# Decay of q moved to the eviction of x^T, weight conversion split over two engines, weight loads paced, second halves of w1 and w2 converted beside the FFN, a group's conversions moved behind the next scores

## The chip, the cores and the metric

One core of a Trainium2 chip. The metric is the device time of one execution in microseconds (us). "Span" is an execution seen by the profiler, 1.6 to 2.2 us shorter than its time (3.5 once).

The engines: TensorE (PE in the profile, PEld its weight loads), VectorE (DVE), ScalarE (ACT), GpSimd (POOL), and SyncE (SP), which here only issues DMAs. "SPq" is SyncE's own instruction queue.

## The reference, cut to what matters

```python
# q, k, v: (8, 8, 576, 64) fp32.   w1, w2: (512, 1024), w3: (1024, 1024), w_out: (1024, 512), all fp64
gamma = 1.0 - 2.0 ** (-5.0 - np.arange(H))
Dmat  = np.where(rel >= 0, gamma[:, None, None] ** rel, 0.0)       # rel = query position - key position
attn  = np.matmul(scale * np.matmul(q, k^T) * Dmat, v)             # linear attention with decay
x     = attn.transpose(0, 2, 1, 3).reshape(4608, 512)
a, b  = x @ w1, x @ w2
out   = ((a * b) @ w3) @ w_out
```

The weights come as fp64 and the kernel computes in fp32, so it rebuilds fp32 numbers from the two 32-bit words of each fp64 value. w3 and w_out have nothing between them, so the kernel multiplies them once: w3o = w3 @ w_out.

## The kernel before

Two stages. In the first, 20 groups (four pairs of batch entries, five chunks of up to 128 positions each) go through attention, and beside it 40 blocks of 128 x 512 weights are loaded as raw fp64 (0.52 MB each), converted, and w3 @ w_out is formed. In the second, the FFN runs over 12 tiles of 384 rows.

The decay is split: k's side multiplies v, q's side multiplies q, both on GpSimd, before TensorE transposes q and k.

```python
def load(g, names):                    # k, q, v of a chunk; pieces of 256 bytes
    ...
        t = ld.tile([P, 2 * H, D], F32, tag="ld_" + nm, bufs={"k": 2, "q": 1, "v": 3}[nm])
        nc.sync.dma_start(t[:sz], src[nm][...])

def front(g):
    for t, gam in ((qn, gq), (vn, gk)):
        nc.gpsimd.tensor_tensor(out=t[:sz], in0=t[:sz], in1=gam[...].to_broadcast([sz, 2 * H, D]), op=ALU.mult)
    # transposes of k and q on TensorE, evicted by ScalarE
    ...
def load_block():                      # a raw fp64 block; three buffers
    t = raw.tile([P, CV, 2], I32, tag="raw", bufs=3)
    nc.sync.dma_start(t, w[...])       # the same SyncE queue as k, q, v
    ...
def convert_block():                   # seven VectorE operations
    ...
    converted[0] += 1
    load_block()                       # refills the buffer that was just freed

for g in range(G):                     # G = 20
    load(g + 2, "kv")
    front(g + 1)
    load(g + 2, "q")
    w3_work(...)                       # transposes and products of w3 that are ready
    convert_up_to(pace[g])             # 2 or 3 blocks a group
    pv(g)                              # attention product, evicted to x^T by ScalarE
    state(g + 1)
    score(g + 1)                       # scores; VectorE multiplies them with the causal mask
```

In the timelines of this case VectorE's operations, and the loads in SyncE's queue, start in the order of the program (those of the changed kernel at 36 to 51 us are shown below).

## Time and profile before

| | |
|---|---|
| time, median (range) | 1050.91 us (1049.49 to 1051.23) |
| first stage / FFN | 303.6 / 746.4 us |
| TensorE busy, first stage | 234.8 us, mean granted clock 0.88 |
| VectorE busy, first stage | 236.5 us |
| share of the 16 DMA engines, first stage | 0.76, at 164 GB/s |

To read it: no engine is full over the first stage as a whole, so the stage is made of stretches with different bounds. The lines are in the prediction below (there and later, a row of 40 digits is the span in 40 equal slices, and a digit the busy share in tenths; PEclk is the granted clock in tenths of full speed; a DMA share can pass 1, as it adds up the times of packets; a line of waits ends with total us, times, and the longest wait).

### The profile page before, as it was taken

The numbers are of one execution on the slowest core, as the hardware profiler recorded it, in microseconds if no ns is written. First come the engines' busy times: TensorE is split into PE (matmuls) and PEld (weight loads), VectorE is DVE, ScalarE is ACT, GpSimd is POOL, SyncE is SP. The second block draws the span as 40 slices with busy tenths as digits, with TensorE's granted clock in tenths as the row PEclk, the third lists the DMA queues.
The fourth block names the chain that finished last, engine by engine and source line by source line (L and its number), as shares of the span: only waits on it lengthen the run. The fifth ranks groups of instructions, "written<-read, shape, count | busy, mean of one in ns | idle before, by whom it ended". The sixth has DMA issues, their size and how long they took to land.

```text
span 1050.1 us, 11351 instructions
## 1 busy us (share of the span) xinstructions
PE 977.6 (93%) x4933; PEld 582.6 (55%) x4933; DVE 290.0 (28%) x475; ACT 146.7 (14%) x285; POOL 82.7 (8%) x47
## 2 busy tenths in 40 slices
PE   3974999886799999999999999999999999999998
PEld 3853655575675455554555555455554545555453
DVE  4898679599821000010100001010010101001010
ACT  2322121232220000000000010000101000000010
POOL 3333121223310000000000000000000000000000
PEclk8887999987899999999999999999999999999999
DMA  9976576699900000000000000000000000000000
GB/s 191 241 164 153 129 160 149 133 213 185 174 4 1 21 10 1 30 1 31 0 13 17 1 30 1 31 0 11 20 1 31 0 21 10 11 20 1 31 0 30
DMA packets 124002, 59.51 MB, mean 57 GB/s; under 512 B 114216, under 2 KB 114216, under 8 KB 123952
## 3 DMA queue, kind: packets, MB, share of 16 engines
q1 hardware_dynamic: 122624, 58.73, 24.0%
q8 instruction: 38, 0.62, 0.3%
q10 hardware_dynamic: 1328, 0.06, 0.1%
q14 instruction: 12, 0.10, 0.0%
HBM read 49.34 MB, written 9.44 MB: 56 GB/s over the span
## 4 chain that ended last, share of the span: by engine, by line
PE 78%; DVE 18%; issue 2%; DMA 1%; SPq 1%; ACTq 0%; ACT 0%; POOL 0%; POOLq 0%; DVEq 0%
PE up L352 47%; PE po L363 24%; PE ps L298 3%; DVE e L267 3%; DVE pm L152 3%; DVE m L272 3%; DVE e L262 2%; DVE e L264 2%; DVE e L265 2%; DVE m L270 2%; DVE w L274 1%; PE xps L197 1%; DVE w_sb L274 1%; PE tp L134 1%; PE tp L290 1%
## 5 line engine op out<-in xcount | busy, mean ns | idle before, releaser
L352 PE MATMUL up<-xT,w_sb 128*128 128x384 f32 x1536 | 497.4, 486 | 0.0
L352 PEld LDWEIGHTS up<-xT,w_sb 128*128 128x128 f32 x1536 | 291.8, 190 | 205.8 <-issue 5.4
L363 PE MATMUL po<-w3o,ab 128*128 128x512 f32 x576 | 249.2, 592 | 0.0
L357 DVE TENSOR_TENSOR ab<-up,a 128x384 f32<-128x384 f32 x96 | 53.5, 558 | 670.6 <-PE up L352 670.6
L363 PEld LDWEIGHTS po<-w3o,ab 128*128 128x128 f32 x576 | 109.4, 190 | 135.2 <-issue 132.0
L356 ACT COPY a<-up 128x384 f32<-128x384 f32 x96 | 46.0, 479 | 416.6 <-PE up L352 416.6
L134 PE MATMUL tp<-ident,ld_q 128*128 128x128 f32 (+1 forms) x160 | 26.7, 311 | 55.6 <-POOL ld_q L123 35.1
L298 PE MATMUL ps<-wo,w3T 128*128 128x512 f32 x128 | 59.6, 622 | 0.0
L366 ACT COPY ot<-po 128x512 f32<-128x512 f32 x36 | 21.1, 586 | 258.9 <-PE po L363 258.9
L123 POOL TENSOR_TENSOR ld_q<-ld_q,gq 128x1024 f32<-128x1024 f32 (+1 forms) x20 | 40.5, 2025 | 207.6 <-DMA ld_q<-in_q_dram 195.6
L152 DVE TENSOR_TENSOR pm<-sc,mask 128x512 f32<-128x512 f32 (+1 forms) x80 | 45.3, 626 | 36.2 <-PE sc L149 36.2
L134 PEld LDWEIGHTS tp<-ident,ld_q 128*128 128x128 f32 (+1 forms) x160 | 20.0, 166 | 60.6 <-POOL ld_q L123 37.9
L197 PE MATMUL xps<-pm,ld_v 128*64 128x128 f32 (+1 forms) x640 | 42.8, 296 | 0.0
L123 POOL TENSOR_TENSOR ld_v<-ld_v,gk 128x1024 f32<-128x1024 f32 (+1 forms) x20 | 42.0, 2101 | 2.9 <-DMA ld_v<-in_v_dram 2.9
L298 PEld LDWEIGHTS ps<-wo,w3T 128*128 128x128 f32 x128 | 25.2, 202 | 29.5 <-issue 29.2
L197 PEld LDWEIGHTS xps<-pm,ld_v 128*64 128x64 f32 (+1 forms) x640 | 38.2, 160 | 5.3 <-issue 5.3
L149 PE MATMUL sc<-qT,kT 64*128 64x128 f32 (+1 forms) x640 | 40.3, 278 | 0.0
L149 PEld LDWEIGHTS sc<-qT,kT 64*128 64x128 f32 (+1 forms) x640 | 36.6, 188 | 1.6 <-issue 0.5
L267 DVE SCALAR_TENSOR_TENSOR e<-raw,e 128x512 int32<-128x512 int32 x40 | 32.4, 811 | 1.4
L272 DVE SCALAR_TENSOR_TENSOR m<-raw,m 128x512 f32<-128x512 uint32 x40 | 29.3, 732 | 1.4
L262 DVE TENSOR_SCALAR e<-raw 128x512 int32<-128x512 int32 x40 | 29.2, 729 | 0.8
L137 ACT COPY qT<-tp 128x512 f32<-128x512 f32 (+1 forms) x40 | 21.3, 550 | 56.7 <-PE tp L134 56.7
(32 smaller groups left out, 307.1 us busy)
## 6 DMA issues: line engine op xcount, KB each, us to landing
raw<-in_moe_w_dram SPq DMA_DIRECT2D x24, 512.0 KB, 4.3
out_dram<-ot SPq DMA_DIRECT2D x36, 256.0 KB, 2.0
ld_k<-in_k_dram SPq DMA_DIRECT2D x16, 512.0 KB, 6.0
ld_v<-in_v_dram SPq DMA_DIRECT2D x16, 512.0 KB, 8.4
ld_q<-in_q_dram SPq DMA_DIRECT2D x16, 512.0 KB, 7.1
raw<-in_moe_w_out_dram SPq DMA_DIRECT2D x8, 512.0 KB, 4.9
raw<-in_moe_w_dram SPq DMA_DIRECT2D x16, 256.0 KB, 5.4
ld_k<-in_k_dram SPq DMA_DIRECT2D x4, 256.0 KB, 4.8
```

Of the source, the lines that this page charges most:

```text
L123: nc.gpsimd.tensor_tensor(out=t[:sz], in0=t[:sz], in1=gam[:sz, c].rearrange("p b h -> p (b h)").unsqueeze(2).to_broadcast([sz, 2 * H, D]), ...
L134: nc.tensor.transpose(tp[:, p, :sz], src[:sz, h:h + 2, :].rearrange("p a d -> p (a d)"), ident[:sz, :sz])
L149: nc.tensor.matmul(sc[j][:sz, p, :sz], kT[hs, b, p, :sz], qT[hs, b, p, :sz], start=True, stop=True)
L152: nc.vector.tensor_mul(pm[:sz, b, j, :, :sz], sc[j][:sz, :, :sz], mask[:sz, :sz].unsqueeze(1).to_broadcast([sz, NP, sz]))
L197: nc.tensor.matmul(banks[r][heads[half], b, n, :sz], vs[:sz, b * H + 2 * p + j, :], pm[:sz, b, j, p, :sz], start=(c == 0 and m == 0), stop ...
L262: vec.tensor_scalar(out=e, in0=hi, scalar1=1, scalar2=21, op0=ALU.logical_shift_left, op1=ALU.logical_shift_right)
L267: vec.scalar_tensor_tensor(e, in0=hi, scalar=-(1 << 31), in1=e, op0=ALU.bitwise_and, op1=ALU.bitwise_or)
L272: vec.scalar_tensor_tensor(m.bitcast(F32), in0=lo.bitcast(U32), scalar=2.0 ** -32, in1=m, op0=ALU.mult, op1=ALU.add)
L298: nc.tensor.matmul(ps, live["w3T", ft][:, g, :], wo[:, g, :], start=(g == 0), stop=(g == KF - 1))
L352: nc.tensor.matmul(t, w[:, c, f * P:(f + 1) * P], xT[:, c, n * TB:(n + 1) * TB], start=(c == 0), stop=(c == KD - 1))
L357: nc.vector.tensor_mul(live["ab", i, n][:, f, :], ps[1], a)
L363: nc.tensor.matmul(po, ab[:, f, t * P:(t + 1) * P], w3o[:, f, :], start=(f == 0), stop=(f == KF - 1))
```

## The change

Its intent: take the multiplication of q off GpSimd (and off the way to TensorE), make VectorE's conversion cheaper, and move part of it out of the first stage.

- GpSimd no longer multiplies q. The decay of q, spread over partitions by eight small TensorE products, is applied when x^T is evicted from PSUM (the memory that TensorE writes its products to), which VectorE now does instead of ScalarE.
- Two of the seven conversion operations become two relus on ScalarE. To let them overlap, a block is begun one ahead of the one being finished.
- The pacing puts 8 blocks into the first 11 groups and 24 into the last 9. The last 8 of the 40 (second halves of w1 and w2) are converted beside the first FFN products.
- The w3 product is cut in two parts around the attention product, and a group's conversions move behind the next group's scores.

```diff
 def front(g):
-    for t, gam in ((qn, gq), (vn, gk)):
-        nc.gpsimd.tensor_tensor(out=t[:sz], in0=t[:sz], in1=gam[...], op=ALU.mult)
+    nc.gpsimd.tensor_tensor(out=vn[:sz]..., in0=vn[:sz]..., in1=gk[...], op=ALU.mult)
 ...
 def pv(g):
-        nc.scalar.copy(live["xT", i][...], banks[r][:, :, :, :sz])
+        nc.vector.tensor_tensor(out=live["xT", i][...], in0=banks[r][:, :, :, :sz], in1=gT[...], op=ALU.mult)
 ...
-    vec.tensor_scalar(out=e, in0=e, scalar1=-896.0, scalar2=0.0, op0=ALU.add, op1=ALU.max)
-    vec.tensor_scalar(out=e, in0=e, scalar1=255.0, scalar2=2.0 ** 23, op0=ALU.min, op1=ALU.mult)
+    nc.scalar.activation(e, e, relu, bias=lim[:, 0:1], scale=-1.0)
+    nc.scalar.activation(e, e, relu, bias=lim[:, 1:2], scale=-2.0 ** 23)
 ...
+    slow, few = G // 2 + 1, KF
+    first = len(blocks) - 2 * KD
+    pace = [few * (g + 1) // slow for g in range(slow)]
+    pace += [few + -(-(first - few) * (g + 1) // (G - slow)) for g in range(G - slow)]
 ...
+    load(0, "kqv")          # now ahead of everything else
 ...
     score(0)
+    decays()                # eight products that spread the decay of q
     for g in range(G):
         load(g + 2, "kv")
         front(g + 1)
         load(g + 2, "q")
-        w3_work((converted[0] - KF) // 2)
-        convert_up_to(pace[g])
+        w3_mm(done, 0)
         pv(g)
+        w3_mm(done, 1)
         state(g + 1)
         score(g + 1)
+        w3_tr(turned[0])
+        convert_up_to(pace[g])
 ...
+    for half in range(2):
+        for n in range(2):
+            for f in range(half * NP, half * NP + NP):
+                up(0, n, f)
+                convert_up_to(converted[0] + 1)
```

More of the change, by code (lines that the diff above doesn't have):

```diff
@@ L73 @@
     w3_part, first_part = ExitStack(), ExitStack()
-    wst = w3_part.enter_context(tc.tile_pool(name="wst", bufs=2))
-    raw, ld, fr = (first_part.enter_context(tc.tile_pool(name=nm, bufs=2, side="right"))
-                   for nm in ("raw", "ld", "fr"))
+    raw = ctx.enter_context(tc.tile_pool(name="raw", bufs=2, side="right"))
+    wst = w3_part.enter_context(tc.tile_pool(name="wst", bufs=1))
+    ld, fr = (first_part.enter_context(tc.tile_pool(name=nm, bufs=2, side="right")) for nm in ("ld", "fr"))
     ctx.enter_context(tc.manual_schedule())
-    ident = const.tile([P, P], F32, tag="ident", name="ident")
-    make_identity(nc, ident)
-    mask = const.tile([P, P], F32, tag="mask", name="mask")
-    nc.vector.memset(mask, 1.0)
-    nc.gpsimd.affine_select(out=mask, in_=mask, compare_op=ALU.is_ge, fill=0.0,
-                            base=0, pattern=[[1, P]], channel_multiplier=-1)
-    gk = const.tile([P, NC, 2, H], F32, tag="gk", name="gk")
-    gq = const.tile([P, NC, 2, H], F32, tag="gq", name="gq")
-    dq = const.tile([H, S], F32, tag="dq", name="dq")
-    nc.scalar.dma_start(dq, decay_q)
-    for c in range(NC):
-        for b in range(2):
-            nc.scalar.dma_start(gk[:sizes[c], c, b, :], decay_k[starts[c]:starts[c] + sizes[c], :])
-    gps = acc.tile([P, NC, H], F32, tag="acc", name="gps")
-    for c in range(NC):
-        nc.tensor.transpose(gps[:sizes[c], c, :], dq[:, starts[c]:starts[c] + sizes[c]], ident[:H, :H])
-    for c in range(NC):
-        for b in range(2):
-            nc.vector.tensor_copy(gq[:sizes[c], c, b, :], gps[:sizes[c], c, :])
-    w1_sb = const.tile([P, KD, DF], F32, tag="w1", name="w1_sb")
-    w3o = const.tile([P, KF, DM], F32, tag="w3o", name="w3o")
-    wo = wst.tile([P, KF, DM], F32, tag="wo", name="wo", bufs=1)
     live = {}
@@ L116, in load, with decays @@
             live[nm, g] = t
+    load(0, "kqv")
+    ident = const.tile([P, P], F32, tag="ident", name="ident")
+    make_identity(nc, ident)
+    mask = const.tile([P, P], F32, tag="mask", name="mask")
+    nc.vector.memset(mask, 1.0)
+    nc.gpsimd.affine_select(out=mask, in_=mask, compare_op=ALU.is_ge, fill=0.0,
+                            base=0, pattern=[[1, P]], channel_multiplier=-1)
+    gk = const.tile([P, NC, H], F32, tag="gk", name="gk")
+    dq = wst.tile([P, DF], F32, tag="w3", name="dq")[:H, :S]
+    nc.scalar.dma_start(gk[:short, 0, :], decay_k[:short, :])
+    nc.scalar.dma_start(gk[:, 1:, :], decay_k[short:, :].rearrange("(c p) h -> p c h", p=P))
+    nc.scalar.dma_start(dq, decay_q)
+    gT = const.tile([P, NP, S], F32, tag="gT", name="gT")
+    lim = const.tile([P, 2], F32, tag="lim", name="lim")
+    nc.vector.memset(lim[:, 0:1], 1151.0)
+    nc.vector.memset(lim[:, 1:2], 255.0 * 2.0 ** 23)
+    def decays():
+        sel = wst.tile([P, KF, P], F32, tag="w3T", name="sel")
+        for p in range(NP):
+            for half in range(2):
+                h = 2 * p + (half ^ (p // 2))
+                nc.vector.tensor_copy(sel[:H, p, heads[half]], ident[:H, h:h + 1].to_broadcast([H, D]))
+        for s0 in range(0, S, S // 2):
+            for p in range(NP):
+                gps = acc.tile([P, S // 2], F32, tag="acc", name="gps")
+                nc.tensor.matmul(gps, sel[:H, p, :], dq[:, s0:s0 + S // 2],
+                                 start=True, stop=True)
+                nc.scalar.copy(gT[:, p, s0:s0 + S // 2], gps)
+    w12h = {nm: [const.tile([P, KD, CV], F32, tag=nm + "a", name=nm + "_sb")] for nm in ("w1", "w2")}
+    w3o = const.tile([P, KF, DM], F32, tag="w3o", name="w3o")
+    wo = wst.tile([P, KF, DM], F32, tag="wo", name="wo")
     def front(g):
@@ L121, in front @@
         kn, qn, vn = live["k", g], live["q", g], live["v", g]
-        for t, gam in ((qn, gq), (vn, gk)):
-            nc.gpsimd.tensor_tensor(
-                out=t[:sz], in0=t[:sz],
-                in1=gam[:sz, c].rearrange("p b h -> p (b h)").unsqueeze(2).to_broadcast([sz, 2 * H, D]),
-                op=ALU.mult)
+        nc.gpsimd.tensor_tensor(
+            out=vn[:sz].rearrange("p (b h) d -> p b h d", b=2), in0=vn[:sz].rearrange("p (b h) d -> p b h d", b=2),
+            in1=gk[:sz, c].unsqueeze(1).unsqueeze(3).to_broadcast([sz, 2, H, D]), op=ALU.mult)
         kT = fr.tile([P, 2, NP, P], F32, tag="kT", name="kT", bufs=1)
@@ L200, in pv @@
         for r in range(2):
-            nc.scalar.copy(
-                live["xT", i][:, 2 * r:2 * r + 2, :, starts[c]:starts[c] + sz].rearrange("p n b s -> p b n s"),
-                banks[r][:, :, :, :sz])
+            s0 = slice(starts[c], starts[c] + sz)
+            nc.vector.tensor_tensor(
+                out=live["xT", i][:, 2 * r:2 * r + 2, :, s0].rearrange("p n b s -> p b n s"),
+                in0=banks[r][:, :, :, :sz],
+                in1=gT[:, 2 * r:2 * r + 2, s0].unsqueeze(1).to_broadcast([P, 2, 2, sz]), op=ALU.mult)
     blocks = []
@@ L208 @@
         blocks.append((("wo", g), moe_w_out, g, 0, lambda g=g: wo[:, g, :]))
+    w12 = [((nm, c, f0), w, c, f0, lambda nm=nm, c=c, f0=f0: w12h[nm][f0 // CV][:, c, :])
+           for f0 in range(0, DF, CV) for nm, w in (("w1", moe_w1), ("w2", moe_w2)) for c in range(KD)]
     for ft in range(KF):
@@ L212 @@
                            lambda ft=ft, g0=g0: w3_tile(ft)[:, g0:g0 + CV]))
-    for nm, w in (("w1", moe_w1), ("w2", moe_w2)):
-        for c in range(KD):
-            for f0 in range(0, DF, CV):
-                blocks.append(((nm, c, f0), w, c, f0,
-                               lambda nm=nm, c=c, f0=f0: w12(nm)[:, c, f0:f0 + CV]))
-    at = {key: n for n, (key, *_) in enumerate(blocks)}
-    loaded, converted = [0], [0]
-    def w12(nm):
-        if nm == "w1":
-            return w1_sb
-        if "w2" not in live:
-            w3_work(KF)
-            w3_part.close()
-            w2p = ctx.enter_context(tc.tile_pool(name="w2p", bufs=1, reuse_waits="tile"))
-            live["w2"] = w2p.tile([P, KD, DF], F32, tag="w2", name="w2_sb")
-        return live["w2"]
+        blocks.append(w12[ft])
+    blocks += w12[KF:]
+    at = {key: n for n, (key, *_) in enumerate(blocks)}
+    loaded, begun, converted, turned = [0], [0], [0], [0]
     def w3_tile(ft):
@@ L250, in load_block, with begin_block @@
         loaded[0] += 1
-    def convert_block():
-        n = converted[0]
+    def begin_block():
+        n = begun[0]
         t = live["raw", n]
         lo, hi = t[:, :, 0], t[:, :, 1]
-        dst = blocks[n][4]()
-        e = raw.tile([P, CV], I32, tag="exp", name="e", bufs=1)
-        m = raw.tile([P, CV], I32, tag="man", name="m", bufs=1)
+        e = raw.tile([P, CV], I32, tag="exp", name="e")
+        m = raw.tile([P, CV], I32, tag="man", name="m")
         vec = nc.vector
@@ L263, in convert_block @@
                           op0=ALU.logical_shift_left, op1=ALU.logical_shift_right)
-        vec.tensor_scalar(out=e, in0=e, scalar1=-896.0, scalar2=0.0, op0=ALU.add, op1=ALU.max)
-        vec.tensor_scalar(out=e, in0=e, scalar1=255.0, scalar2=2.0 ** 23,
-                          op0=ALU.min, op1=ALU.mult)
-        vec.scalar_tensor_tensor(e, in0=hi, scalar=-(1 << 31), in1=e,
-                                 op0=ALU.bitwise_and, op1=ALU.bitwise_or)
+        relu = mybir.ActivationFunctionType.Relu
+        nc.scalar.activation(e, e, relu, bias=lim[:, 0:1], scale=-1.0)
+        nc.scalar.activation(e, e, relu, bias=lim[:, 1:2], scale=-2.0 ** 23)
         vec.tensor_scalar(out=m, in0=hi, scalar1=0x000FFFFF, scalar2=0x00100000,
@@ L273, in convert_block, with end_block @@
                                  op0=ALU.mult, op1=ALU.add)
-        vec.scalar_tensor_tensor(dst, in0=m.bitcast(F32), scalar=2.0 ** -20,
+        live["em", n] = e, m
+        begun[0] += 1
+    def end_block():
+        n = converted[0]
+        hi = live["raw", n][:, :, 1]
+        e, m = live["em", n]
+        vec = nc.vector
+        vec.scalar_tensor_tensor(e, in0=hi, scalar=-(1 << 31), in1=e,
+                                 op0=ALU.bitwise_and, op1=ALU.bitwise_or)
+        vec.scalar_tensor_tensor(blocks[n][4](), in0=m.bitcast(F32), scalar=2.0 ** -20,
                                  in1=e.bitcast(F32), op0=ALU.mult, op1=ALU.mult)
@@ L279, in convert_up_to @@
     def convert_up_to(n):
-        while converted[0] < min(n, len(blocks)):
-            convert_block()
+        n = min([n, len(blocks)] + [at["w3", ft, 0] for ft in range(KF) if ft > turned[0]])
+        while converted[0] < n:
+            while begun[0] < min(converted[0] + 2, len(blocks)):
+                begin_block()
+            end_block()
     def w3_tr(ft):
-        convert_up_to(at["w3", ft, DF - CV] + 1)
         t = wst.tile([P, KF, P], F32, tag="w3T", name="w3T")
@@ L291, in w3_tr, with w3_mm, w3_ready @@
                                     ident)
-            (nc.scalar.copy if i == 0 else nc.vector.tensor_copy)(t[:, i:i + NP, :], tp)
+            nc.scalar.copy(t[:, i:i + NP, :], tp)
         live["w3T", ft] = t
-    def w3_mm(ft):
-        ps = acc.tile([P, DM], F32, tag="acc", name="ps")
-        for g in range(KF):
+    def w3_mm(ft, part):
+        if part == 0:
+            live["w3ps"] = acc.tile([P, DM], F32, tag="acc", name="ps")
+        ps = live["w3ps"]
+        for g in range(part * NP, part * NP + NP):
             nc.tensor.matmul(ps, live["w3T", ft][:, g, :], wo[:, g, :],
                              start=(g == 0), stop=(g == KF - 1))
-        nc.scalar.copy(w3o[:, ft, :], ps)
-    w3_steps = [(w3_tr, 0)]
-    for ft in range(KF):
-        w3_steps += [(w3_tr, ft + 1), (w3_mm, ft)] if ft + 1 < KF else [(w3_mm, ft)]
-    def w3_work(rows):
-        while w3_steps and (w3_steps[0][1] < rows):
-            fn, ft = w3_steps.pop(0)
-            fn(ft)
-    pace = [2 * (g + 1) for g in range(4)]
-    while len(pace) < G:
-        pace.append(min(pace[-1] + (3 if pace[-1] < KF + 2 * KF else 2), len(blocks)))
-    load(0, "kqv")
-    load_block()
+        if part == 1:
+            nc.scalar.copy(w3o[:, ft, :], ps)
+    def w3_ready(ft):
+        return ft < KF and converted[0] > at["w3", ft, DF - CV]
+    slow, few = G // 2 + 1, KF
+    first = len(blocks) - 2 * KD
+    pace = [few * (g + 1) // slow for g in range(slow)]
+    pace += [few + -(-(first - few) * (g + 1) // (G - slow)) for g in range(G - slow)]
     load(1, "kv")
@@ L322 @@
     load(1, "q")
-    load_block()
     state(0)
     score(0)
+    decays()
+    load_block()
+    load_block()
+    done = 0
     for g in range(G):
@@ L332 @@
             load(g + 2, "q")
-        w3_work((converted[0] - KF) // 2)
-        convert_up_to(pace[g])
+        if done < turned[0]:
+            w3_mm(done, 0)
         pv(g)
+        if done < turned[0]:
+            w3_mm(done, 1)
+            done += 1
         if g + 1 < G:
@@ L338 @@
             score(g + 1)
-    w2_sb = live["w2"]
+        if w3_ready(turned[0]):
+            w3_tr(turned[0])
+            turned[0] += 1
+        convert_up_to(pace[g])
     first_part.close()
-    ffn = ctx.enter_context(tc.tile_pool(name="ffn", bufs=2, reuse_waits="tile"))
+    while done < KF:
+        if done < turned[0]:
+            w3_mm(done, 0)
+            w3_mm(done, 1)
+            done += 1
+        if w3_ready(turned[0]):
+            w3_tr(turned[0])
+            turned[0] += 1
+    w3_part.close()
+    w2nd = ctx.enter_context(tc.tile_pool(name="w2nd", bufs=1, side="right", reuse_waits="tile"))
+    for nm in ("w1", "w2"):
+        w12h[nm].append(w2nd.tile([P, KD, CV], F32, tag=nm + "b", name=nm + "_sb"))
+    ffn = ctx.enter_context(tc.tile_pool(name="ffn", bufs=2, side="right", reuse_waits="tile"))
     def up(i, n, f):
@@ L346, in up @@
         if f == 0:
-            live["ab", i, n] = ffn.tile([P, KF, TB], F32, tag="ab", name="ab")
+            live["ab", i, n] = ffn.tile([P, KF, TB], F32, tag="ab", name="ab", bufs=3)
         ps = []
-        for w in (w1_sb, w2_sb):
+        half, f1 = divmod(f * P, CV)
+        for nm in ("w1", "w2"):
+            w = w12h[nm][half]
             t = acc.tile([P, TB], F32, tag="acc", name="up")
             for c in range(KD):
-                nc.tensor.matmul(t, w[:, c, f * P:(f + 1) * P], xT[:, c, n * TB:(n + 1) * TB],
+                nc.tensor.matmul(t, w[:, c, f1:f1 + P], xT[:, c, n * TB:(n + 1) * TB],
                                  start=(c == 0), stop=(c == KD - 1))
@@ L368, in down @@
         nc.sync.dma_start(out[r:r + P, :], ot)
+    for half in range(2):
+        for n in range(2):
+            for f in range(half * NP, half * NP + NP):
+                up(0, n, f)
+                convert_up_to(converted[0] + 1)
     every = [(i, n) for i in range(NB2) for n in range(NB)]
@@ L373 @@
         for f in range(KF):
-            if m == 0 or f > 0:
+            if m > 1 and f > 0:
                 up(i, n, f)
-        if m + 1 < len(every):
+        if 0 < m < len(every) - 1:
             up(*every[m + 1], 0)
```

## The prediction

> **What bounds the kernel now.** I read the page's slices first, then the busy table by stage, then the chain that ended last in order of time, then the VectorE and GpSimd timelines.
>
> ```profile
> PE   3974999886799999999999999999999999999998
> DVE  4898679599821000010100001010010101001010
> PEclk8887999987899999999999999999999999999999
> DMA  9976576699900000000000000000000000000000
> ```
>
> There are two stages: attention with weight preparation in the first 11 to 12 slices, and an FFN of solid TensorE. The chain gives the border, and what the FFN costs:
>
> ```profile
> 303.62 46.64 PE up L352 x144
> 350.25 20.60 PE po L363 x48
> 370.85 41.28 PE up L352 x128
> ```
>
> One FFN tile is 41.28 + 20.60 = 61.9 us; twelve are 742.6. The busy table by stage (columns: stretch, its length, busy us and instruction count of PE, PEld, DVE, ACT, POOL, then granted clock, DMA share, GB/s) says the same:
>
> ```profile
> 0.00:303.60 303.60, 234.80 (x2822) 181.46 (x2822) 236.47 (x379) 78.68 (x152) 82.72 (x47) 0.88 0.76 164
> 303.60:1050.00 746.40, 742.77 (x2114) 401.14 (x2112) 53.52 (x96) 67.99 (x134) 0.00 (x0) 1.00 0.03 13
> ```
>
> The FFN (746.4 us, clock 1.00) has the same matmuls after the change, so it is a floor. All gain must come out of the first 303.6 us. There nothing is full on average: VectorE is busy 236 us of 304, TensorE 235 at a mean clock of 0.88, the DMA 0.76. The page's chain names VectorE's conversion for most of that stage (DVE 18% of the span is 189 us). A piece of VectorE's and of GpSimd's timeline shows why:
>
> ```profile
> 257.03 0.43 DVE L264 TENSOR_SCALAR e<-e 128x512 int32<-128x512 int32 x1
> 257.50 2.00 DVE L265 TENSOR_SCALAR e<-e 128x512 int32<-128x512 int32 x1
> 259.54 2.27 DVE L267 SCALAR_TENSOR_TENSOR e<-raw,e 128x512 int32<-128x512 int32 x1
> 261.73 0.41 DVE L270 TENSOR_SCALAR m<-raw 128x512 int32<-128x512 int32 x1
> 262.18 0.69 DVE L272 SCALAR_TENSOR_TENSOR m<-raw,m 128x512 f32<-128x512 uint32 x1
> ```
> ```profile
> 257.31 1.91 POOL L123 TENSOR_TENSOR ld_q<-ld_q,gq 128x1024 f32<-128x1024 f32 x1 [10.27 <-DMA ld_q<-in_q_dram]
> 259.18 2.08 POOL L123 TENSOR_TENSOR ld_v<-ld_v,gk 128x1024 f32<-128x1024 f32 x1
> ```
>
> The operation that takes 0.43 us takes 2.00 while GpSimd multiplies q; the next, 0.69 alone, takes 2.27 while it multiplies v. TensorE, which needs the scaled q for its transposes, waits behind the same operation:
>
> ```profile
> PEld tp L134 <- POOL ld_q L123: 37.9, 13, 5.4
> POOL ld_q L123 <- DMA ld_q<-in_q_dram: 195.6, 18, 23.5
> ```
>
> **What the Trainium skill says.** (1) "SBUF — State Buffer", section "Who interferes with whom": GpSimd's ports are VectorE's second pair, and a VectorE instruction in a two-port mode, or one with two SBUF inputs, is blocked while GpSimd has them; one with a single SBUF input outside these modes is not. The trace agrees on both: 0.43 becomes 2.00, while the mask multiplication (PSUM and one SBUF input) took 2.48 us for four both at 293.01 us, beside a GpSimd operation, and at 299.82, without one. (2) "VectorE: DVE Perf Modes", "The perf-mode tier table": fp32 in SBUF doubles for tensor_scalar and not for two-input forms. Agrees: 0.41 to 0.43 against 0.69 us. (3) "TensorE: Matmul & The Clock Gate", "What's actually happening": an idle window of about 3.4 us halves the clock. Agrees: in 99 to 110 us the granted clock is 0.5 for 10.2 us after gaps of 4.16 and 4.79 us. (4) "ScalarE: Activation LUTs", "What ACT_TABLE_LOAD costs": an activation with a pointer bias takes about 280 ns + 0.833 ns an element, 0.71 us for 512. No run before has one; the page adds, under "Table sets", that relu is in every set, so I expect no new table load.
>
> **The change part by part, first on VectorE, then on the path.**
>
> Conversion now: the seven groups total 29.2 + 21.8 + 20.2 + 32.4 + 21.9 + 29.3 + 35.8 (the last three groups of L274) = 190.6 us for 40 blocks, 4.77 a block. Undisturbed in the timeline a block is 0.41 + 0.43 + 0.43 + 0.69 + 0.42 + 0.69 + 0.69 = 3.76. So GpSimd's 40 operations cost VectorE 40 x 1.01 = 40 us.
> - Two of the seven operations go to ScalarE: 3.76 - 0.86 = 2.90 a block undisturbed.
> - 8 of 40 blocks go beside the FFN: 32 x 2.90 = 93 us remain in the first stage.
> - Half of GpSimd's operations (q) go: the stall falls from 40 to about 20 us (my halving).
> - The eviction of x^T comes to VectorE: 40 operations from PSUM with one SBUF input, of the form of the mask multiplication, 0.626 mean: +25 us. The mask multiplication stays at 45 us; eight evictions of w3^T (5.5 us) leave.
> - Sum: 93 + 20 + 25 + 45 = 183 us, against 236.
>
> ScalarE's first stage: 79 - 20 (x^T) + 5 (w3^T) + 3 (eight decay evictions) + 64 x 0.71 = 112 us. Not a bound.
>
> TensorE's first stage at full clock, from the last groups of the chain: a middle chunk is transposes 1.90, state product 1.03, attention product 1.90, state 0.93, scores 1.99 = 7.75 us; the last of a head pair lacks the state, 6.8; the first is short, I put it at 5. Four times (5 + 3 x 7.75 + 6.8) = 140. The w3 product adds eight times (6.87 + 0.89) = 62. Sum 202: the 235 busy hold some 30 of half clock.
>
> DMA: 49.3 MB are read now, 4.2 MB of which (8 blocks of 0.52) move. Where it is full the windows give about 220 GB/s (219 at 36 to 39 us, 219 at 270 to 276). 45.1 MB / 220 = 205 us.
>
> So VectorE stops being the bound, and TensorE at 202 and the DMA at 205 are equal. They do not bound the same groups, though. The pacing converts 8 blocks in the first 11 of 20 groups and 24 in the last 9, with all of the w3 product in those.
> - First 11 groups: chunks 0 to 12 of q, k, v (10 x 1.57 + 3 x 0.79 = 18.1 MB) and 11 raw blocks (5.8 MB): 23.9 MB / 220 = 109 us. TensorE has only 77 us (11/20 of 140), so this half is bound by loads. A single q buffer allows at most one group per q load (landing 7.1 us in the page) plus transposes (1.0) and issue (up to 2), 9 to 10 us, much the same. I put its end at 112 us.
> - Last 9 groups and the rest of w3: TensorE 63 + 62 = 125 us; VectorE 24 x 2.90 + 9 x 3.7 + about 12 of stall = 115; DMA 21 MB, 96 us. TensorE bounds, and I add 16 us for waits and half clock, half of what the stage has now. 141 us.
> - First stage: 112 + 141 = 253 us, 50 less.
>
> FFN: the first eight half-width products take 8 x 2.58 = 20.6 us of TensorE, then the second halves must be there. VectorE needs for them 8 x (2.90 + 0.56) = 27.7 us plus the first 3 us until there is anything to evict, less the 1.5 us that is begun ahead: 29 us. The last slice of w2 is wanted at 22.8, so TensorE loses 6 us; with the raw ring of three (4.3 to 5.4 us a landing against 3.5 us a block) and a half clock after it, 10 us. So 756 us.
>
> Sum: 253 + 756 = 1009, plus 1 of difference between span and time: **1010 us**, -3.9%.
>
> **The rivals.**
> (a) The loads take the place of VectorE for good: q, k, v in 256-byte pieces, one q buffer, and a queue whose raw loads stand in program order ahead of the next k and v and wait on VectorE. For: DMA tenths of 9 in the first slices and again near 230 to 280 us, GpSimd's 195.6 us of waiting for q. Against: those waits include the time VectorE and TensorE held the buffer up. If the first half runs at 11.5 us a group and the second is held too: first stage 275, total 1032, -1.8%.
> (b) The second halves hold up the FFN more than I think, because evictions, conversion and loads run in one ordered queue. For: VectorE needs more time there than TensorE. Against: it ends after eight blocks. Each 1 us a block is 8 us; with half clock 25 us instead of 10: 1025.
> (c) ScalarE in order: its relus wait for VectorE and stand ahead of the next transposes' evictions, tying TensorE to VectorE again. For: program order. Against: 112 us of work in 253, and 6 to 14 us of TensorE work between them. Worth 10 to 15 us: 1022.
> (d) The stall by GpSimd falls to nearly nothing and the clock stays up: first stage 235, total 993.
>
> **Range and chances.** (a) and (d) set the ends: 993 to 1032. 2% faster is below 1029.9, which needs a first stage and FFN stall together 20 us worse than my sum; two of the three bad rivals would have to come true together. Faster 0.86, within 2% 0.13, slower 0.01, as no part adds work to the TensorE floor. Range 994 to 1031.
>
> **What would show it.** First stage ends (first up product) near 253 us; half 1 near 112 us with DMA tenths of 9; the w3 product wholly after that, TensorE tenths of 9. VectorE 183 us before the FFN, its operations of 2 us only beside multiplications of v. Relus 64 before the FFN at about 0.7 us and one table load. No wait of the q transposes on GpSimd. One TensorE gap of 6 to 10 us some 21 us into the FFN, then tiles of 61.9 us again. A first stage over 275 us, or a gap over 25 us, would prove me wrong; so would x^T evictions much over 0.63 us.

## More of the kernel before

One line is shown here. It is SyncE's own queue, with total us, times, and the longest wait:

```profile
SPq L248 <- DVE m L272: 92.8, 23, 12.0
```

L248 is the load of a raw block, and what it waits for is the conversion on VectorE that frees the buffer.

## The result, and the profile after

| | before | changed |
|---|---|---|
| time, median (range) | 1051.07 us (1049.49 to 1051.49) | 1048.49 us (1047.93 to 1050.36) |
| first stage (first FFN product) | 303.6 us | 300.3 us |
| FFN | 746.4 us | 746.4 us |
| VectorE busy, first stage | 236.5 us | 164.6 us |

Ratios here are the mean time of one kernel's runs over that of the other's of the same rounds, so not quite the ratio of the medians. This one is 0.9981, with a 95% interval of 0.9964 to 0.9999: the same. I had predicted 1010 us, with 994 to 1031 as the range. (The table of the kernel before, above, has its first three runs; here a fourth is added.) 72 us of VectorE's work are gone from the first stage, and the stage is 3 us shorter.

The slices of the changed kernel:

```profile
PE   6987677979899999999999999999999999999998
DVE  0545448574946100010100001010010101001010
PEclk9988877989999999999999999999999999999999
DMA  9589587867422000000000000000000000000000
```

The chain that ended last, by engine:

```profile
PE 88%; DMA 6%; SPq 2%; DVE 2%; ACT 1%; issue 0%; POOL 0%; ACTq 0%; POOLq 0%
```

VectorE has gone from 18% of it to 2%. In its place stand TensorE (78% before), and what was 1% each: loads (6%) and the queue that issues them (2%). VectorE's row no longer has a run of 8s and 9s, so it isn't the bound. But TensorE's is no fuller, its clock still falls, and the DMA's row swings: a 5 between 9s. The prediction had asked for steady 9s in the first half.

I split the stage where step 11 of the loop begins (the 14th load of k, which is issued two groups ahead). That is at 150 us; the prediction put the end of this half at 112. The busy table by stage of the changed kernel, columns as in the prediction:

```profile
0.00:150.00 150.00, 110.46 (x1586) 98.45 (x1588) 62.51 (x124) 46.94 (x87) 25.63 (x20) 0.86 0.79 157
150.00:300.30 150.30, 129.08 (x1251) 87.03 (x1248) 102.07 (x171) 64.30 (x108) 13.37 (x7) 0.93 0.66 157
300.30:1046.70 746.40, 742.61 (x2113) 401.66 (x2111) 73.51 (x133) 77.67 (x147) 0.00 (x0) 1.00 0.05 17
```

In the first half nothing is full: TensorE 110 of 150 us, VectorE 63, and the DMA moves 157 GB/s although it reaches more where it is fed (260 GB/s from 48 to 52 us). Cut into slices of 1 us, 39 of these 150 have under 30 GB/s. So neither an engine nor the DMA's rate bounds this half. Something does not ask in time.

SyncE's timeline shows what (start, duration, the load issued):

```profile
36.20 0.37 SPq L91 DMA_DIRECT2D ld_q<-in_q_dram  x1
47.08 0.34 SPq L252 DMA_DIRECT2D raw<-in_moe_w_out_dram  x1
47.52 0.38 SPq L91 DMA_DIRECT2D ld_k<-in_k_dram  x1
47.95 2.72 SPq L91 DMA_DIRECT2D ld_v<-in_v_dram  x1
50.77 3.31 SPq L91 DMA_DIRECT2D ld_q<-in_q_dram  x1
```

Between 36.57 and 47.08 us the queue issues nothing. The next in line is a raw weight block, and k, v and q of a later group stand behind it. VectorE's timeline of the same time:

```profile
41.15 2.48 DVE L166 TENSOR_TENSOR pm<-sc,mask 128x512 f32<-128x512 f32 x4 [0.94 <-PE sc L163]
...
45.75 0.69 DVE L273 SCALAR_TENSOR_TENSOR m<-raw,m 128x512 f32<-128x512 uint32 x1
46.36 0.69 DVE L283 SCALAR_TENSOR_TENSOR e<-raw,e 128x512 int32<-128x512 int32 x1
47.09 0.69 DVE L285 SCALAR_TENSOR_TENSOR wo<-m,e 128x512 f32<-128x512 f32 x1
```

The last operation that reads the raw buffer (L283) ends at 47.05, and 0.03 us later the load goes out. That conversion stands behind the mask multiplication, which waited for the scores. And the DMA meanwhile, then TensorE some us later:

```profile
42.00:48.00 6.00, 5.77 (x114) 5.29 (x112) 5.90 (x12) 3.93 (x7) 0.08 (x1) 1.00 0.00 0
```
```profile
48.40 2.06 PE L163 MATMUL sc<-qT,kT 64*128 64x128 f32 x32 [0.62 <-ACT qT L151]
54.71 1.94 PE L148 MATMUL tp<-ident,ld_k 128*128 128x128 f32 x8 [4.26 <-DMA ld_k<-in_k_dram]
58.96 1.94 PE L148 MATMUL tp<-ident,ld_q 128*128 128x128 f32 x8 [2.31 <-DMA ld_q<-in_q_dram]
```

The DMA moves nothing for 6 us (0.00 share, 0 GB/s). Then three loads are issued at once, TensorE has no work from 50.5 to 54.7 waiting for k, then again for q; its transposes take 1.94 us where 1.04 to 1.09 is normal, as the granted clock was 0.50 from 54 us on, after the gap. This recurs about every second group. The waits of SyncE's queue in the first 150 us add it up:

```profile
SPq L252 <- DVE e L283: 45.4, 5, 10.4
```

Five stops, 45 us. Over the whole first stage this wait is 112.3 us, 22 times; the one of the kernel before is 92.8 us, 23 times.

### The profile page after: what moved, and what is told of

It is laid out like the page before. It is cut to its first block, busy times and chain, and to the rows that moved or that the text cites. A ratio compares the mean times of both kernels' runs of the same rounds, so it can differ in the third digit from the quotient of the medians. Undisturbed runs are those within 1.5% of the kernel's fastest.

```text
span 1046.7 us, 11348 instructions
## 1 busy us (share of the span) xinstructions
PE 982.2 (94%) x4944; PEld 587.1 (56%) x4944; DVE 238.1 (23%) x427; ACT 188.9 (18%) x341; POOL 39.0 (4%) x27
## 3 DMA queue, kind: packets, MB, share of 16 engines
q1 hardware_dynamic: 122624, 58.73, 23.9%
## 4 chain that ended last, share of the span: by engine, by line
PE 88%; DMA 6%; SPq 2%; DVE 2%; ACT 1%; issue 0%; POOL 0%; ACTq 0%; POOLq 0%
PE up L385 47%; PE po L396 24%; DMA ld_q<-in_q_dram 6%; PE ps L314 6%; PE xps L211 3%; PE tp L148 3%; PE sc L163 2%; SPq L91 2%; PE xps L204 2%; PE st L184 1%; DVE pm L166 1%; PE gps L124 1%; DMA ld_v<-in_v_dram 1%; DVE m L273 0%; DVE e L283 0%
## 5 line engine op out<-in xcount | busy, mean ns | idle before, releaser
L396 PEld LDWEIGHTS po<-w3o,ab 128*128 128x128 f32 x576 | 109.6, 190 | 135.0 <-issue 131.8
L166 DVE TENSOR_TENSOR pm<-sc,mask 128x512 f32<-128x512 f32 (+1 forms) x80 | 45.6, 629 | 46.9 <-PE sc L163 46.8
L148 PE MATMUL tp<-ident,ld_k 128*128 128x128 f32 (+1 forms) x160 | 23.8, 301 | 25.1 <-DMA ld_k<-in_k_dram 25.1
L138 POOL TENSOR_TENSOR ld_v<-ld_v,gk 128x1024 f32<-128x1024 f32 (+1 forms) x20 | 38.1, 1903 | 224.4 <-DMA ld_v<-in_v_dram 176.8
L268 ACT ACTIVATE e<-e,lim 128x512 int32<-128x512 int32 x40 | 28.9, 724 | 86.9 <-DVE e L265 86.9
L163 PE MATMUL sc<-qT,kT 64*128 64x128 f32 (+1 forms) x640 | 41.3, 283 | 2.8 <-ACT qT L151 2.8
L216 DVE TENSOR_TENSOR xT<-xps,gT 128x512 f32<-128x512 f32 (+1 forms) x40 | 23.6, 632 | 75.2 <-PE xps L211 75.2
L148 PEld LDWEIGHTS tp<-ident,ld_q 128*128 128x128 f32 (+1 forms) x160 | 22.5, 177 | 31.2 <-issue 30.1
L211 PE MATMUL xps<-pm,ld_v 128*64 128x128 f32 (+1 forms) x640 | 39.7, 283 | 0.0
L211 PEld LDWEIGHTS xps<-pm,ld_v 128*64 128x64 f32 (+1 forms) x640 | 35.2, 151 | 4.8 <-issue 4.3
L148 PEld LDWEIGHTS tp<-ident,ld_k 128*128 128x128 f32 (+1 forms) x160 | 19.3, 160 | 27.9 <-issue 24.7
## 6 DMA issues: line engine op xcount, KB each, us to landing
out_dram<-ot SPq DMA_DIRECT2D x36, 256.0 KB, 2.0
raw<-in_moe_w_dram SPq DMA_DIRECT2D x16, 256.0 KB, 3.9
ld_k<-in_k_dram SPq DMA_DIRECT2D x4, 256.0 KB, 6.1
```

The source lines that it names most:

```text
L138: nc.gpsimd.tensor_tensor(out=vn[:sz].rearrange("p (b h) d -> p b h d", b=2), in0=vn[:sz].rearrange("p (b h) d -> p b h d", b=2), in1=gk[: ...
L148: nc.tensor.transpose(tp[:, p, :sz], src[:sz, h:h + 2, :].rearrange("p a d -> p (a d)"), ident[:sz, :sz])
L163: nc.tensor.matmul(sc[j][:sz, p, :sz], kT[hs, b, p, :sz], qT[hs, b, p, :sz], start=True, stop=True)
L166: nc.vector.tensor_mul(pm[:sz, b, j, :, :sz], sc[j][:sz, :, :sz], mask[:sz, :sz].unsqueeze(1).to_broadcast([sz, NP, sz]))
L211: nc.tensor.matmul(banks[r][heads[half], b, n, :sz], vs[:sz, b * H + 2 * p + j, :], pm[:sz, b, j, p, :sz], start=(c == 0 and m == 0), stop ...
L268: nc.scalar.activation(e, e, relu, bias=lim[:, 0:1], scale=-1.0)
```

## The experiments

**Theory 1 (queue order):** a raw load that waits for VectorE holds the k, v and q loads behind it in SyncE's in-order queue. The change put the conversions behind the next scores, which makes that wait longer, and this gave back what the cheaper conversion had gained. **Theory 2:** the single q buffer, with the rate of loads in 256-byte pieces, sets the pace; the queue's order doesn't matter.

Each experiment is one edit of the kernel that it is told against (e5 to e7 and e10 to e12 stand on earlier ones), run three rounds plus a profiled run. e1 to e4 ran on one chip, e5 to e8 on a second, e9 to e12 on a third; the kernel before ran in each of these batches (medians 1051.6, 1051.3 and 1050.5 us), the changed kernel was not run again. "First half" is where the 14th load of k is issued, "stage" where the first FFN product starts, both in the profiled run.

| run | time, median us | ratio to before | first half | stage |
|---|---|---|---|---|
| kernel before | 1050 to 1052 | 1 | 209.4 | 303.6 |
| changed kernel | 1048.5 | 0.998 | 149.9 | 300.3 |
| e1 raw load after k, v, q | 1004.0 | 0.955 | 110.7 | 256.0 |
| e2 no blocks in the first half | 1029.5 | 0.979 | 105.3 | 283.1 |
| e3 decays early | 1044.5 | 0.993 | 143.1 | 296.3 |
| e4 conversions before attention | 999.9 | 0.951 | 114.9 | 252.9 |
| e5 = e4 + e3 | 994.4 | 0.946 | 108.5 | 244.8 |
| e6 = e4, exponents on VectorE | 1011.2 | 0.961 | 118.8 | 263.3 |
| e7 = e4, GpSimd multiplies q | 1009.4 | 0.960 | 125.6 | 264.2 |
| e8 before, raw load after k, v, q | 1040.3 | 0.990 | 192.5 | 293.1 |
| e9 before, conversions late | 1125.1 | 1.070 | 264.3 | 376.9 |
| e10 = e5, no blocks beside the FFN | 1010.6 | 0.961 | 111.3 | 263.2 |
| e11 = e5, even pace | 995.1 | 0.947 | 135.0 | 246.3 |
| e12 = e11, raw load after k, v, q | 1046.2 | 0.996 | 164.9 | 296.6 |

(The halves of the kernel before hold other shares of the weights, so its 209.4 is to be compared with e8 and e9 only, and e11's 135.0 holds more of them than e5's.)

### e1: the raw load after the next k, v and q

```diff
         converted[0] += 1
-        load_block()
+        owed[0] += 1                  # paid at once only in the FFN, or if a conversion needs it
 ...
         load(g + 2, "q")
+        pay()                         # load_block() for every block owed
```

> One change to the changed kernel: the load that refills a raw weight buffer is no longer issued right after the conversion that frees it, but after the next group's k, v and q loads. Theory 1 (queue order: the raw load waits on VectorE in the in-order queue and holds the next k, v, q behind it, so that the DMA stands idle 39 of the first 157 us): the first w3 product starts 25 to 45 us earlier than 179 us, the first FFN product well before 300 us, time 1005 to 1025 us. Theory 2 (the single q buffer and the rate of 256-byte pieces set the pace, the queue's order does not matter): time within 5 us of 1048.

1004.0 us (1000.5 to 1006.3): 44 us less than the changed kernel, by the order of the loads alone. No engine has more or less to do. The first half ends at 110.7 us, and the table by stage now shows a DMA that is full over it:

```profile
0.00:110.70 110.70, 95.65 (x1528) 85.38 (x1528) 60.90 (x119) 43.43 (x83) 23.94 (x20) 0.97 1.03 207
```

Of these 111 us, 6 have under 30 GB/s, where the changed kernel had 39 of 150. In SyncE's queue the raw loads wait 10.0 us for VectorE over this half, against 47.1 in the first 150 us of the changed kernel (the line of 45.4 and one of 1.7). Theory 1 holds, and Theory 2 falls: the q buffer is single here too. The first w3 product starts at 141.4 us instead of 179.0, 38 us earlier, as expected; the time is 1 us below the range I gave.

### e2: no block converted in the first 11 groups

```diff
-    slow, few = G // 2 + 1, KF
+    slow, few = G // 2 + 1, 0
```

(and one more `convert_up_to(first)` in the loop that finishes the w3 product)

> One change to the changed kernel: no block is converted in the first 11 groups, all 32 in the last 9 and at the end of the stage. No raw load then stands between the loads of q, k, v in the first half. Theory 1 (queue order): those 11 groups go at 8 to 9.5 us each, group 11 begins near 110 us instead of 157; the second half gets longer by 15 to 30 us as its work is pushed together; time 1010 to 1040 us. Theory 2 (q buffer, rate of small pieces): the 11 groups still take 12 us or more each, group 11 begins after 140 us, and the time is 1055 us or more.

1029.5 us. From the third to the 14th load of k it is 8.2 us a group (14.98 to 105.25 us, eleven groups), where the changed kernel takes 12.25 (15.20 to 149.94). A group without raw loads in front of it is not held, with the same q buffer and the same small pieces. The second half gets 27 us longer (105.3 to 283.1 us is 177.8, against 150.4), as expected. So this is no better way to mend it, but it speaks against Theory 2 a second time. It is the weaker of the two, as the first half also moves eight raw blocks (4.2 MB, about 20 us at the 207 GB/s of e1) fewer.

### e3: the products that spread the decay, earlier

```diff
+    decays()
     state(0)
     score(0)
-    decays()
```

> One change to the changed kernel: the eight products that spread the decay of q over the partitions (8.0 us of TensorE at 15.9 us) are issued before the first state product instead of after the first scores, where TensorE waits for v anyway. If these 8 us lie on the path: 3 to 6 us less, 1042 to 1045. If the loads' queue sets the pace and absorbs them: within 1.5 us of 1048.

1044.5 us (1043.7 to 1044.9), 4 us less. The eight products take 8.0 us of TensorE. In the changed kernel they ran from 15.9 to 24 us, the q transposes of group 1 after them, and so the third q load went out at 27.5 us. My prediction had not counted them at all. Small, but on the path.

### e4: conversions before the attention product

```diff
         load(g + 2, "q")
+        convert_up_to(pace[g])
         w3_mm(done, 0)
         pv(g)
 ...
         w3_tr(turned[0])
-        convert_up_to(pace[g])
```

(and `convert_up_to(first)` after the loop and in the loop that finishes w3)

> One change to the changed kernel: the conversions of a group are issued before its attention product, where the kernel before had them, not after the next scores. Theory 1 (queue order): the raw loads are freed about 5 us earlier in each group, so the next k, v, q are issued earlier and the first half gets 15 to 35 us shorter, unless the mask multiplications that now stand behind the conversions take some back; time 1020 to 1040. Theory 2: no gain, 1045 to 1060.

999.9 us (998.7 to 1001.7), 49 us less: more than expected, and as much as e1 by the other end of the same wait. Here the order of the loads is untouched; what a raw load waits for comes earlier, and in the first 115 us raw loads wait 10.9 us for VectorE, none of them for the operation of the 45.4 us. The two halves:

```profile
0.00:115.00 115.00, 95.04 (x1493) 84.78 (x1494) 63.43 (x120) 45.60 (x85) 23.84 (x19) 0.95 1.02 203
115.00:252.90 137.90, 130.72 (x1343) 89.82 (x1342) 101.44 (x174) 65.33 (x110) 16.48 (x8) 0.97 0.72 172
```

First the DMA is full (1.02 of its share, 203 GB/s), then TensorE (130.7 of 137.9 us). Those are the two bounds that the prediction named, and 115 + 138 = 253 us is the stage that it had computed. In part that is luck. TensorE has 225.8 us of busy time here against a computed 202 (8 of them the decay's products, which the sum left out), and the first half moves 203 GB/s against 220; in the second half the 16 us that I had added for waits took this up (130.7 busy of 137.9 us, where I had 125 of 141).

### e5: e4 and e3 together

> Conversions before the attention product and the spreading of the decay early, both at once. With the queue's hold gone the first 11 groups are bound by the loads' rate; the 8 us of products at the start delay the third q load (issued after them at 27.5 us while the DMA was idle from 24 to 28), so if that idle stretch counts now, 3 to 6 us less than the 999.9 of the conversions alone: 994 to 997 us. If the loads catch up: 998 to 1000.

994.4 us (992.9 to 996.4), the fastest that I ran: 5.4% under the kernel before.

### e6, e7: two parts of the change undone on e4

e6 puts the two exponent operations back on VectorE:

```diff
-    nc.scalar.activation(e, e, relu, bias=lim[:, 0:1], scale=-1.0)
-    nc.scalar.activation(e, e, relu, bias=lim[:, 1:2], scale=-2.0 ** 23)
+    vec.tensor_scalar(out=e, in0=e, scalar1=-896.0, scalar2=0.0, op0=ALU.add, op1=ALU.max)
+    vec.tensor_scalar(out=e, in0=e, scalar1=255.0, scalar2=2.0 ** 23, op0=ALU.min, op1=ALU.mult)
```

> Conversions before the attention product, and the two exponent operations back on VectorE (all seven there, 3.76 us a block instead of 2.90). 32 x 0.86 = 28 us more of VectorE before the FFN. If VectorE has room there, as its 0.6 to 0.8 of busy says, 1000 to 1006 us; if its conversions sit on the path again, up to 28 us: 1015 to 1028.

1011.2 us (1006.1 to 1014.3), 11 more. That lies between the two cases I had set out (up to 1006, from 1015): of 28 us of VectorE work about 40% reach the end.

e7 lets GpSimd multiply q by ones, so that the result stays right:

```diff
+    nc.gpsimd.tensor_tensor(out=qn[:sz]..., in0=qn[:sz]..., in1=one[...].to_broadcast([sz, 2, H, D]), op=ALU.mult)
     kT = fr.tile(...)
```

> Conversions before the attention product, and GpSimd multiplies q by ones before the transposes, which puts back the operation that the change removed (but keeps the decay in the eviction of x^T). 20 operations of 1.9 us on the path from q's landing to its transposes, and they block VectorE's two-port and two-input operations. If my reading of the kernel before was right, 10 to 35 us more: 1010 to 1035. If the removal was worth nothing: 1000 to 1004.

1009.4 us, 9.5 more, just under what I expected (10 to 35). The wait that the change had removed is back:

```profile
PEld tp L153 <- POOL ld_q L143: 23.7, 9, 6.5
```

So both parts are worth about 1% each once the loads flow. In e7 the wait before the transposes and the longer blocking of VectorE come back together, and the run does not part them. No run takes either part out of the changed kernel as it was, so what they are worth there is not shown.

### e8, e9: the same two levers on the kernel before

e8 defers the raw loads in the kernel before, as e1 does in the changed one.

> The kernel before, with one change: the refill of a raw weight buffer is issued after the next group's k, v and q loads instead of right after the conversion. If the queue's order held up the kernel before as well (its DMA idles 50 of the first 205 us and the queue waits 92.8 us for VectorE): 15 to 35 us less, 1016 to 1036. If VectorE and GpSimd were its bound, as I predicted: within 8 us of 1051.

1040.3 us, 11 less (ratio 0.990), between the two cases. The queue's order did cost the kernel before something, and mending it this way gives a quarter of what it gives in the changed one. That is a net figure: VectorE now waits for raw blocks that come later, 27.1 us in all, most of it in this line, which the kernel before does not have:

```profile
DVE e L271 <- DMA raw<-in_moe_w_dram: 23.5, 7, 7.1
```

So how much of its first stage came from the order alone is not shown.

e9 moves the conversions of the kernel before to where the changed kernel has them, and changes nothing else:

```diff
         w3_work((converted[0] - KF) // 2)
-        convert_up_to(pace[g])
         pv(g)
         state(g + 1)
         score(g + 1)
+        convert_up_to(pace[g])
```

> The kernel before, with one change: a group's conversions are issued after the next group's scores, where the changed kernel has them, instead of before the attention product. If that place and the queue's order together are what ate the gain, the kernel before must lose by it too: 15 to 45 us more, 1066 to 1096. If the place does no harm without the rest of the change: within 8 us of 1051.

1125.1 us, 74 more, far above the 15 to 45 expected. The line of SyncE's queue has grown from 92.8 to:

```profile
SPq L248 <- DVE m L272: 162.4, 26, 20.3
```

This is the other half of the evidence. The new place of the conversions, taken alone, costs 74 us here, where a group converts two or three blocks before the queue can go on.

### e10: all blocks before the FFN

On e5. The second halves are written over the first ones, since there is no room for both, so the result is wrong; the work and the traffic are those of a kernel without the split.

```diff
-    first = len(blocks) - 2 * KD
+    first = len(blocks)
 ...
-    ... lambda nm=nm, c=c, f0=f0: w12h[nm][f0 // CV][:, c, :])
+    ... lambda nm=nm, c=c, f0=f0: w12h[nm][0][:, c, :])
```

> On the kernel of 994.4 us (conversions before the attention product, decays early): all 40 blocks are converted before the FFN. The second halves are written over the first ones, as there is no room for them, so the result is wrong on purpose; work and traffic are the same. 8 x 2.90 = 23 us more of VectorE and 4.2 MB more of loads (19 us at 220 GB/s) in the stage. If loads or VectorE bound it: 10 to 25 us more, 1004 to 1020. If TensorE bounds the second half and hides them: within 5 us of 994.

1010.6 us, 16 more than e5, within the first case. In the profile VectorE waits 26.6 us for raw blocks, against 15.2 in e5, and raw loads are 4% of the chain that ended last, so it is the loads that show here. Of the three parts of the change that I undid (e6, e7, e10), this one is worth most.

### e11, e12: an even pace

e11 spreads the 32 blocks evenly over the groups, on e5:

```diff
-    pace = [few * (g + 1) // slow for g in range(slow)]
-    pace += [few + -(-(first - few) * (g + 1) // (G - slow)) for g in range(G - slow)]
+    pace = [-(-first * (g + 1) // G) for g in range(G)]
```

> On the kernel of 994.4 us: the 32 blocks are spread evenly over the 20 groups (1.6 each) instead of 8 in 11 and 24 in 9, so that the w3 product falls into groups where TensorE waits for loads. With loads at about 220 GB/s as the only bound the stage is 45.1 MB / 220 = 205 us and some 15 of start and end, against 244.8 now: 965 to 985 us. If the loads of the first half, already full there, are what is pushed out: 990 to 1005.

995.1 us: my main expectation (965 to 985) missed, the other case came. The first half's loads were full already, so more raw blocks there push k, v and q out; what the first half loses (135.0 against 108.5 us) the second gains. On this kernel nothing is won by undoing the uneven pace of the change; on the changed kernel as it was this was not run.

e12 adds e1's deferral to that.

> As the even pace, and the refill of a raw buffer is issued after the next k, v and q loads. If the queue's order still costs something where conversions stand before the attention product (the queue waits about 90 us for VectorE in the kernel of 999.9 us): 3 to 12 us less than the even pace alone. If not, within 3 us of it, or a few us more as the raw loads come later.

1046.2 us, 51 more, where I had expected 3 to 12 less. At the even pace the two mends don't add up; they fight (with the change's own pace the pair was not run). With the conversions early in the group, a raw load that is issued just before them comes too late, and now VectorE waits for it:

```profile
DVE e L274 <- DMA raw<-in_moe_w_dram: 88.2, 14, 10.6
```

In e5 the same wait was 15.2 us. e8 has the same wait, smaller. I read this from the waits; no run here takes it apart further (a fourth raw buffer might).

## Why the prediction was wrong, point by point

- **The FFN as a floor:** right. 746.4 us in both.
- **The stall in the FFN (10 us):** wrong, it is 0. I took 2.58 us for one first-layer product pair, dividing the group's 41.28 us by 16. A tile has 8 of them, and 128 instructions, so each is 16 instructions and 41.28 / 8 = 5.16 us: the trace lists two matmul instructions for each fp32 matmul of the program. The first eight take 41.3 us, more than the 29 us that I had VectorE need. The chain of the changed kernel has the first two tiles in one piece, twice 41.28 us, without a gap:

```profile
300.35 82.56 PE up L385 x256
382.91 20.60 PE po L396 x48
```

- **VectorE's first stage (183 us):** 62.5 + 102.1 = 164.6. The term that was off most is GpSimd's stall, for which I halved 40 to 20 us. From the means against the undisturbed durations it is (0.775 - 0.692 + 0.729 - 0.685 + 0.474 - 0.418) x 40 = 7 us. I halved for GpSimd's operations only, and forgot that two of the seven VectorE operations and 8 of the 40 blocks also get out of its way: 40 x 1/2 x 2.90/3.76 x 32/40 = 12 us would have been the estimate. e6, with all seven operations, bears the halving out: its groups total 165.0 us, which is 15 more than 40 x 3.76, where 40 x 1/2 x 32/40 gives 16. The eviction of x^T, at 0.632 us each, was right.
- **ScalarE (112 us, relus 0.71 us, no new table load):** 46.9 + 64.3 = 111.2 us, 0.724 us, one table load. Right.
- **No more wait of q's transposes on GpSimd:** right; bringing the operation back costs 9.5 us in a kernel whose loads flow (e7).
- **The first 11 groups end at 112 us, bound by the loads' rate:** this is the step that failed. They ended at 150, with the DMA at 157 GB/s and idle for 39 us. The bytes and the rate were near: with the hold gone, e1 and e4 end this half at 111 and 115 us, at 207 and 203 GB/s, which is 22.9 and 23.3 MB against the 23.9 MB at 220 that I had computed. What I left out is that the loads must also be *issued* in time: five stops of the queue at a raw load, 45.4 us. Rival (a) had the mechanism in so many words (raw loads in the queue ahead of the next k and v, waiting on VectorE), gave 11.5 us a group where 12.25 was measured, and I set it aside because part of those waits seemed to be the buffers' own. And I did not ask what moving the conversions behind the scores does to that queue, though the diff shows it.
- **The second half, 141 us:** 150 in the changed kernel; 136 to 145 in e1, e4 and e5.
- **The decay's products:** not in my sum at all; 8 us on TensorE, 4 on the path (e3).
- **Rival (c), ScalarE's relus tie TensorE to VectorE:** no sign of it. ScalarE has 1% of the chain of the changed kernel, and e4 without the relus (e6) is slower.
- **Sums and readings to correct:** rival (a) at 1032 us alone lies above the 1029.9 that counts as 2% faster, so that one rival was enough and no two had to come true together; the 0.86 for "faster" was too high. Rival (d) adds up to 235 + 756 + 1 = 992, not 993. Of the 189 us of VectorE in the chain, about 27 are the mask multiplication, not conversion. The second of the two gaps named with the halved clock (4.79 us) began when the clock was already at 0.50, so only the first shows the fall. And the mask multiplication at 293.01 us ran beside GpSimd for 0.84 of its 2.48 us only.

The difference to the prediction, in spans: 38 us in the first half and 9 in the second, minus the 10 of the FFN that did not come, make 37; measured 1046.7 against 1009, 38.

So the expected gain was not missing. It was there and was given back: the conversion got cheaper, and in the same change it was put where the load queue has to wait for it. e9 shows the price of the place without the rest (+74 us on the kernel before), e4 the gain of the rest without the place (-51 us, ratio 0.951). What stays open is how much of e4's gain would be left if its place and the deferral could be had together with more raw buffers; e12 shows only that with three, at an even pace, they can't.

## What to carry to other kernels

In this kernel a raw load that waited for its buffer held the k, v and q loads behind it, five times for 45.4 us in the first half. When a change moves the work that frees a buffer, ask where the refill stands in the issuing queue and what is behind it, and look at that queue's own waits as you would at an engine's. Their sum does not say what they cost: 92.8 us of them in the kernel before were worth 11 us net when the order was changed (e8), 45.4 us in the first half of the changed kernel and 112.3 in its first stage were worth 44 (e1). When every engine has room and the DMA's row swings between idle and full, look for loads that are issued late, not for bandwidth.

## What the Trainium skill lacked or had wrong

- "DMA: Bandwidth & Descriptors", section "Issuing engines are not separate DMA queues", says that issuing from several engines only saves the sequencer's issue time. I found no page that warns of the other cost of one queue: a load at its head that waits for a semaphore. Here that stopped the queue five times for 45.4 us in the first 150, and reordering alone (e1) gave 44 us. No run here issued from a second engine, so what that would give isn't shown.
- "SBUF — State Buffer", section "Who interferes with whom", is right on which VectorE operations GpSimd blocks (0.43 us became 2.00), but gives no way to size it for a program. With half the GpSimd operations the stall was 15 us of 40 where VectorE kept all its seven operations for 32 of the 40 blocks (e6), and 7 where it had five (the changed kernel).
- "FP8 and Floating Point Precision", section "TensorE Precision Notes", gives four passes for fp32. The durations fit it: a product of 384 columns is two instructions of 0.3225 us, so 4 x 384 columns take 0.645 us. No page that I read says that a trace lists two instructions for one fp32 matmul (16 for the 8 of an up product here), which cost me a factor of two in the time of the first eight up products.
